# A Retention, MoE and feed-forward kernel: ring depth, task distances and forced work changed

## The chip, the cores and the metric

The kernel runs on one core of one Trainium2 chip. The metric is the device time of one execution in microseconds (us). Its engines are TensorE (PE for matmuls, PEld for its weight loads), VectorE (DVE), ScalarE (ACT), GpSimd (POOL) and SyncE (SP), which issues all DMAs here.

## What is computed

Three layers follow each other: Retention over 4 batches, 8 heads, 576 positions and 64 dims; a soft mixture of 8 experts whose mixing matrix P is normalised eight times by rows and columns; and a feed-forward layer with a leaky rectifier.

```python
ret = (1 / sqrt(64)) * (q @ k.T) * Dmat        # Dmat[i, j] = gamma_h ** (i - j), 0 above the diagonal
x = (ret @ v)                                  # 2304 tokens x 512
P = exp(x @ w_gate - max)
for _ in range(8):
    P /= P.sum(1, keepdims=True) + 1e-09
    P /= P.sum(0, keepdims=True) + 1e-09
    P *= N / E
x = sum(P[:, e:e + 1] * (maximum(x @ w1[e], 0) @ w2[e]) for e in range(8))   # 512 -> 1024 -> 512
h = x @ w_in                                   # 512 -> 2048
out = maximum(0.01 * h, h) @ w_out             # 2048 -> 512
```

## The kernel before

**Retention.** 20 chunks (`N`, loop over `n`) of 128 or 64 positions for two heads' halves. Each iteration loads q, k, v three and two chunks ahead, makes the scores on TensorE, multiplies them with the decay table on DVE (L640), adds the state's part, takes absolute values on ACT (L668) and sums them over a ones matrix. From that sum DVE makes a scale row `s` (L708), a power of two, and scales the output (L710). `keep_row` (L715) stores the row to memory two iterations later; `s` is a tile of a ring, two deep by its pool. POOL makes sums and differences of the scaled output (`emit_operands`), ACT and DVE split each into two 16-bit parts.

**Units.** The hidden width is cut into 20 units of 512 columns: 16 for the experts, 4 for the last layer (`NU1`, `NU`). A unit `u` goes over three stages `s` of 384 row pairs; a stage has 14 first products (`product_h`, seven in each of two halves `g`) and 15 groups of second products (`group_s`), which run 20 products behind. Every product is Strassen-like: seven products of operand sums, each of three matmuls on 16-bit parts. Units 0 and 15 (`PLAIN`) make their second products without it.

**Weights.** `prep_steps(u)` makes the tasks for a unit's weights: magnitudes, a scale (`top`, `scale`), scaling by it, then four `split`s: key `("w1", 0)` and `("w1", 1)` for the two halves of the first weights, `("w2",)` for both of the second. A split is twelve tasks: two casts on ACT, two differences and four sums on POOL, two casts on ACT, two differences on POOL. Unit 0's first weights are made during Retention, one task at a time from `step()`, of which an iteration has four. Its magnitudes are maxima on DVE and its scale uses a ones matrix; the other units take sums of magnitudes on ACT, transpose the column total on TensorE, take the maximum and broadcast it.

**The order.** Nothing is scheduled on the chip: `Order` writes the order of instructions at build time with a model of time. A task takes a fixed part and a part per element there, by engine (`COST`, L43); a gate step, entered with 1500 elements on DVE, is 1.75 us. Tasks lie in six queues; `pump` runs after each product and looks at the first 12 tasks of each queue (48 of "turn"). It emits those that are `ready`: every task they need has a modelled end at least `lat` back, their condition holds, their engine is nearly free. `flush` forces tasks whose time has come; `need` does it for weights, `need_x` for operands of a stage, `need_hid` for hidden values.

```python
def flush(self, name, want):
    q = self.queues[name]
    while any(want(x.key) for x in q):
        self.emit(q.pop(0))
```

So a forced task takes all that stands ahead of it in its queue with it. A half of the first weights has the condition `w1_free(g)`: the tile that it writes must have been read for the last time, for `g == 1` by the first half of the last stage of the unit before.

**Gate and layer change.** After the logits of the last stage, 11 tasks (`gate_steps`) normalise P on DVE, each with a product on TensorE for column sums. They must be done before unit 2's second products begin. After unit 15, `turn_steps` scales each row block on POOL (L1261), transposes it on TensorE (`turned`, L1271) and makes the operands of the last layer from it. In the last layer the leaky rectifier of two of the hidden blocks is one ACT instruction (`bent`, called from `splits` at L1057).

Of the kernel before, what the change touches and what calls it, by code (L numbers as in the profile page):

```python
# [8 lines left out]
F32 = mybir.dt.float32  # L9
F16 = mybir.dt.float16  # L10
BF16 = mybir.dt.bfloat16
# [19 lines left out]
ST = 384  # L31
# [4 lines left out]
WS = lambda u: 2.0 ** 13 if u else 2.0 ** 11  # L36
# [27 lines left out]
class Order:  # L64
# [43 lines left out]
    def flush(self, name, want):  # L108
        q = self.queues[name]
        while any(want(x.key) for x in q):  # L110
            self.emit(q.pop(0))
# [3 lines left out]
def retention_moe_ffn_kernel(ctx: ExitStack, tc: tile.TileContext, qk, vk, wg, wm, wf,  # L115
# [53 lines left out]
    def prep_steps(u, small_bank):  # L169
# [3 lines left out]
        def begin():  # L173
            st["iw"] = small.tile([P, 2], F32, tag="iw", name=f"iw{u}")
            st["m"] = small.tile([P, 2], F32, tag="m1f", name=f"m{u}") if u else \
                small.tile([P, 2], BF16, tag="m1b", name=f"m{u}", bufs=1)
# [3 lines left out]
        def amax(part, c):  # L180
            def f():
                nc.vector.tensor_reduce(st["mx"][:, part, c:c + 1], raws[u, part][:, 512 * c:512 * c + 512],
                                        axis=AX.X, op=ALU.max, apply_absolute_value=True)
            return f
# [6 lines left out]

        def top(p):
            def f():
                if u == 0:
                    nc.vector.reduce_max(st["m"][:, p], st["mx"][:, p], axis=AX.X)
                    return
                nc.vector.reduce_sum(st["m"], st["mx"], axis=AX.X)
                bk = small_bank(f"wt{u}")
                for part in range(2):
                    nc.tensor.matmul(bk[:1, P * part:P * part + P], st["m"][:, part:part + 1], ident,  # L200
                                     start=part == 0, stop=True, skip_group_check=True)
                st["r"] = small.tile([1, 2], F32, tag="mrw", name=f"mr{u}", bufs=1)
                nc.vector.reduce_max(st["r"], bk[:1, :2 * P].rearrange("p (a i) -> p a i", a=2), axis=AX.X)
            return f

        def scale(p):
            def f():
                bk = small_bank(f"ws{u}_{p.start}")[:, p]
                if u:
                    nc.tensor.matmul(bk, ones[:1, :], st["r"], start=True, stop=True)  # L210
                else:
                    nc.tensor.matmul(bk, ones_b, st["m"][:, p], start=True, stop=True)
                pow2(st["s"][:, p], bk, f"w{u}_{p.start}")
                recip2(st["iw"][:, p], st["s"][:, p])
                for part in range(p.start, p.stop):
                    s2 = st["s", part] = small.tile([P, 1], F32, tag=f"s2{part}", name=f"sw{u}_{part}", bufs=2)
                    nc.vector.tensor_scalar(s2, st["s"][:, part:part + 1], WS(u), None, op0=ALU.mult)
                if p.stop == 2:
                    fu = small.tile([P, 1], F32, tag="fu", name=f"fu{u}")
                    nc.vector.scalar_tensor_tensor(fu, st["iw"][:, 0:1], 1.0 / (XS * WS(u) ** 2 * HS), st["iw"][:, 1:2],  # L220
                                                   op0=ALU.mult, op1=ALU.mult)
                    wfac[u] = fu
            return f
# [69 lines left out]
        def maxes(part, key):  # L293
            there = None if u == 0 else lambda: (u, part) in raws and order.t >= raw_at[u, part] + 8
            return [add("A" if u else "D", 512, (mags if u else amax)(part, c), (first_,), key, there) for c in range(4)]

        def scaled(p, mx_, key):
            t_ = add("D", 40 if u == 0 else 400, top(p), mx_, key)
            return add("D", 500, scale(p), (t_,), key, lat=0.8)
# [46 lines left out]
        last0 = split(0, 0, pre0[0:2], ka, w1_free(0))  # L346
        pre1 = scales(1, sc, k2)
        last1 = split(1, 0, pre1[0:2], k2, w2_free) + split(1, 1, pre1[2:4], k2, w2_free)
        after(1, last1, k2)
        last0 += split(0, 1, pre0[2:4], kb, w1_free(1))  # L350
        after(0, last0, kb)
# [190 lines left out]
    with ExitStack() as actx:  # L542
# [146 lines left out]
        def emit_scale(n, bank=None):  # L689
# [9 lines left out]
            if c < 4:  # L699
# [3 lines left out]
                sv = s_t = awk.tile([P, P], F32, tag="s", name=f"s{n}")  # L703
# [71 lines left out]
        pre = prep_steps(0, lambda name: misc[0][:, 500:502] if misc[0] else idle_bank(name))  # L775
        wait, drain = [0], []
        emit_qk(0)
        for n in range(N):
# [19 lines left out]
            def step():  # L798
                wait[0] -= 2
                if n >= 4 and pre and pre[0].key == (0, "w1", 1) and wait[0] <= 0:  # L800
                    x = pre.pop(0)
                    wait[0] = {40: 8, 500: 4}.get(x.n, 2)
                    x.f()
                    x.done = 0.0
# [46 lines left out]
        misc[0] = None  # L851
# [89 lines left out]
    def bent(out_, in_, u, scale=1.0):  # L941
        if u < NU1:
            nc.scalar.activation(out_, in_, AF.Relu, scale=scale)
        else:
            nc.scalar.activation(out_, in_, AF.Prelu, scale=scale, alpha=SLOPE)

# [61 lines left out]
    def splits(u, s, g, what):  # L1008
# [45 lines left out]
        elif what == 1:  # L1054
            d = (evac[7], evac[3])
            if not moe:
                d = (add("A", 2 * ST, lambda: bent(fp[:, 1:3], fp[:, 1:3], u), d),)  # L1057
# [176 lines left out]
    def turn_steps(s, j0):  # L1234
# [52 lines left out]
        t = [add("AD", 512, turned(j, h), (b[h],) + p.get(f"x{h}", ()), 0.5) for h in range(2)]  # L1287
# [62 lines left out]
    for n, (u, s) in enumerate(stages):  # L1350
# [95 lines left out]
```

## Time and profile before

| | us |
|---|---|
| median of 3 runs | 1872.95 (1871.28 to 1875.13) |
| profiled execution | 1871.14 |
| its span, first to last instruction | 1869.4 |
| PE busy | 1798.8 (96%) |
| DVE busy | 1486.7 (80%) |
| ACT busy | 1262.1 (68%) |
| POOL busy | 814.7 (44%) |
| mean granted TensorE clock | 0.985 |

The share of busy time is a mean over stages. TensorE's own waits, its granted clock and what released each wait are read stretch by stretch. A granted clock of 1.00 is 2.4 GHz; a stretch below it ran partly at 1.2 GHz.

### The profile page before, as it was taken

To read this page: it belongs to the slowest core of one execution; us is meant where nothing else is said; L and a number is where in the kernel's file an instruction comes from. 1 tells how busy PE (TensorE), PEld (TensorE's weight loads), DVE (VectorE), ACT (ScalarE), POOL (GpSimd) and SP (SyncE) were. 2 spreads that over 40 slices of the span, in tenths; PEclk is the share of its full clock that TensorE was granted. 3 is DMA by queue.
4 is the path that set the end of the run, shared out by engine and by line. 5 is a ranking of instruction groups with operands and counts; after the bars stand their busy time and mean duration, and the time that the engine had idled before them with its cause. 6 is when DMAs were issued, how large, how long until landed. Compare 5 with 4: busy or idle time off the path is not lost.

```text
span 1869.4 us, 35931 instructions
## 1 busy us (share of the span) xinstructions
PE 1798.8 (96%) x13794; PEld 1301.0 (70%) x13794; DVE 1486.7 (80%) x2578; ACT 1262.1 (68%) x2645; POOL 814.7 (44%) x786
## 2 busy tenths in 40 slices
PE   8889999999999999999999999999999988999997
PEld 7744477777777777777777777777765556677776
DVE  7845587988988897988889898988766886597875
ACT  5656677677776767777776767676665666777653
POOL 4734362543525362544535352543227853263500
PEclk9899999999999999999999999999999999999999
DMA  8873353534454553544454453544433534344242
GB/s 321 302 249 102 121 152 122 182 114 150 147 165 135 156 161 118 182 127 148 140 177 132 142 169 123 175 134 129 125 114 104 184 118 142 116 116 148 83 121 77
DMA packets 207857, 276.67 MB, mean 148 GB/s; under 512 B 13874, under 2 KB 177860, under 8 KB 202564
## 3 DMA queue, kind: packets, MB, share of 16 engines
q1 hardware_dynamic: 207684, 274.37, 46.9%
q8 instruction: 108, 1.77, 0.4%
q14 instruction: 65, 0.53, 0.1%
HBM read 244.69 MB, written 29.63 MB: 147 GB/s over the span
## 4 chain that ended last, share of the span: by engine, by line
PE 81%; DVE 9%; POOL 4%; ACT 3%; DMA 2%; issue 2%; SPq 0%; DVEq 0%; ACTq 0%; POOLq 0%
PE s L1125 15%; PE hB L955 11%; PE hA L955 11%; PE s1a L1125 11%; PE hE L955 11%; PE s1b L1125 10%; PE hD L955 5%; DVE y L1138 2%; PE s L1167 2%; POOL raw L260 1%; DVE hs L1046 1%; PE s1b L1167 1%; PE s1a L1167 1%; DMA s_dram<-s 1%; POOL y L1261 1%
## 5 line engine op out<-in xcount | busy, mean ns | idle before, releaser
L955 PEld LDWEIGHTS <-w 128*128 128x128 f16 x5040 | 492.1, 98 | 269.5 <-issue 14.1
L1125 PEld LDWEIGHTS <-hs 128*128 128x128 f16 x3888 | 380.6, 98 | 92.9 <-DVE hs L1046 7.9
L1125 PEld LDWEIGHTS <-hp 128*128 128x128 f16 x2916 | 285.9, 98 | 90.6 <-issue 13.9
L253 POOL TENSOR_TENSOR w<-raw,w 128x384 f16<-128x384 f32 x152 | 164.5, 1096 | 331.2 <-ACT w L243 306.2
L260 POOL TENSOR_TENSOR raw<-raw 128x256 f32<-128x256 f32 x304 | 285.1, 938 | 20.2
L955 PE MATMUL hE<-x,w 128*128 128x384 f16 x1440 | 276.1, 328 | 5.2 <-DMA x<-x 2.8
L1138 DVE SCALAR_TENSOR_TENSOR y<-s,fac,y 128x256 f32<-128x256 f32 (+1 forms) x324 | 197.6, 612 | 102.4 <-PE s L1125 87.1
L955 PE MATMUL hB<-x,w 128*128 128x384 f16 x1440 | 275.1, 327 | 3.2 <-ACT hB L965 3.1
L955 PE MATMUL hA<-x,w 128*128 128x384 f16 x1440 | 276.8, 327 | 0.7 <-DMA x<-x 0.7
L1125 PE MATMUL s<-w,hs 128*128 128x256 f16 x1944 | 265.8, 273 | 1.0 <-ACT s L1143 1.0
L1046 DVE TENSOR_TENSOR hs<-fs,hs 128x768 f16<-128x768 f32 (+1 forms) x228 | 244.1, 1086 | 11.8 <-ACT hs L1036 11.6
L278 POOL TENSOR_TENSOR w<-raw,w 128x512 f16<-128x512 f32 x148 | 191.3, 1308 | 92.7 <-ACT w L272 92.4
L406 POOL TENSOR_TENSOR f<-f,e 128x256 f32<-128x256 f32 x64 | 53.4, 834 | 401.8 <-DVE e L398 393.3
L1036 ACT ACTIVATE hs<-fs 128x768 f16<-128x768 f32 (+1 forms) x228 | 187.6, 823 | 43.9 <-DVE fs L1071 24.6
L1036 ACT ACTIVATE hp<-fp 128x384 f16<-128x384 f32 x240 | 159.3, 678 | 27.6 <-DVE fp L994 20.4
L1138 DVE SCALAR_TENSOR_TENSOR y<-s1b,fac,y 128x512 f32<-128x512 f32 (+1 forms) x163 | 99.7, 612 | 51.1 <-ACT s L1143 22.3
L1125 PE MATMUL s1a<-w,hp 128*128 128x256 f16 x972 | 133.9, 274 | 6.5 <-DVE y L1138 3.5
L955 PE MATMUL hD<-x,w 128*128 128x384 f16 x720 | 139.7, 329 | 0.1
L1125 PE MATMUL s1a<-w,hs 128*128 128x256 f16 x972 | 134.8, 274 | 4.9 <-DVE hs L1046 3.7
L1125 PE MATMUL s1b<-w,hs 128*128 128x256 f16 x972 | 134.0, 273 | 5.1 <-ACT hs L1036 3.2
L1138 DVE SCALAR_TENSOR_TENSOR y<-s1a,fac,y 128x256 f32<-128x256 f32 (+1 forms) x161 | 98.3, 611 | 47.0 <-ACT s L1143 28.9
L1125 PE MATMUL s1b<-w,hp 128*128 128x256 f16 x972 | 132.7, 273 | 2.6 <-DVE y L1138 2.6
(198 smaller groups left out, 2689.9 us busy)
## 6 DMA issues: line engine op xcount, KB each, us to landing
x<-x SPq DMA_DIRECT2D x420, 384.0 KB, 4.1
raw<-in_wm SPq DMA_DIRECT2D x32, 1024.0 KB, 5.1
r<-in_wf SPq DMA_DIRECT2D x64, 256.0 KB, 2.8
qk<-in_qk SPq DMA_DIRECT2D x16, 512.0 KB, 5.9
vk<-in_vk SPq DMA_DIRECT2D x16, 512.0 KB, 5.2
wf_s<-f SPq DMA_DIRECT2D x32, 256.0 KB, 2.7
raw<-wf_s SPq DMA_DIRECT2D x8, 1024.0 KB
x<-xst SPq DMA_DIRECT2D x30, 256.0 KB, 2.0
```

Of the source, the lines that this page charges most:

```text
L253: nc.gpsimd.tensor_tensor(v[0], v[1], v[2], op=ALU.subtract)
L260: nc.gpsimd.tensor_tensor(o, x, y_, op=ALU.subtract)
L278: (nc.gpsimd if u or part else nc.vector).tensor_tensor(lo, r, hi, op=ALU.subtract)
L406: nc.gpsimd.tensor_tensor(dst, dst, cur["tx"].bitcast(F32), op=ALU.mult)
L955: nc.tensor.matmul(bank, w[:, a, wi, k, :], x[:, :, b, k, :], start=r in (1, 5) and k == q == 0, stop=k == 1 and q == 2, skip_group_check= ...
L1036: nc.scalar.activation(hid[k][:, 0, a:b], src[:, a:b], AF.Relu if moe and relu else AF.Copy)
L1046: nc.vector.tensor_tensor(t[:, 1, a:b], src[:, a:b], t[:, 0, a:b], op=ALU.subtract)
L1125: nc.tensor.matmul(out_, t[:, a, i, ts], w[:, b, wi, 0, :], start=start and k == 0, stop=k == 5, skip_group_check=True)
L1138: nc.vector.scalar_tensor_tensor(out_, bank, f, out_, op0=ALU.mult, op1=ALU.add)
L1167: nc.tensor.matmul(bank, t[:, a, i, ts], w[:, b], start=l == g == q == 0, stop=l == g == 1 and q == 2, skip_group_check=True)
L1261: nc.gpsimd.tensor_scalar(y[i], y[i], st["s", j][:, h:h + 1], None, op0=ALU.mult)
```

## The change

Seven edits. (1) The ring of Retention's scale rows is four deep. (2) Unit 0's weights are made as the other units' are, with magnitudes on ACT, and a task of them leaves `step()` once what it needs is two steps back (three for the maximum and the broadcast), chosen among the first six. (3) `top` is cut in two: the total on DVE (`total`), then transpose and maximum 0.6 us later in the model; the broadcast waits 1.2 instead of 0.8 us. (4) Gate steps wait 4.0 us of modelled time instead of 1.0. (5) The transposes at the layer change wait 1.5 instead of 0.5. (6) `flush` forces only the wanted tasks and what they depend on, and the second half of the first weights is queued ahead of the second weights. (7) The leaky rectifier of two blocks goes to ACT or DVE, whichever the model has free.

```diff
-WS = lambda u: 2.0 ** 13 if u else 2.0 ** 11
+WS = 2.0 ** 13
     def flush(self, name, want):
-        q = self.queues[name]
-        while any(want(x.key) for x in q):
-            self.emit(q.pop(0))
+        for x in list(self.queues[name]):
+            if want(x.key):
+                self.force(x)
+
+    def force(self, x):
+        for q in self.queues.values():
+            if x in q:
+                for d in x.deps:
+                    self.force(d)
+                q.remove(x)
+                self.emit(x)
+                return
...
+        def total(p):
+            def f():
+                nc.vector.reduce_sum(st["m"][:, p], st["mx"][:, p], axis=AX.X)
+            return f
         def top(p):
             def f():
-                if u == 0:
-                    nc.vector.reduce_max(st["m"][:, p], st["mx"][:, p], axis=AX.X)
-                    return
-                nc.vector.reduce_sum(st["m"], st["mx"], axis=AX.X)
-                bk = small_bank(f"wt{u}")
-                for part in range(2):
-                    nc.tensor.matmul(bk[:1, P * part:P * part + P], st["m"][:, part:part + 1], ident,
-                                     start=part == 0, stop=True, skip_group_check=True)
+                bk = small_bank(f"wt{u}_{p.start}")
+                n = p.stop - p.start
+                for i in range(n):
+                    nc.tensor.matmul(bk[:1, P * i:P * i + P], st["m"][:, p.start + i:p.start + i + 1], ident,
+                                     start=i == 0, stop=True, skip_group_check=True)
...
-            return [add("A" if u else "D", 512, (mags if u else amax)(part, c), (first_,), key, there) for c in range(4)]
+            return [add("A", 512, mags(part, c), (first_,), key, there) for c in range(4)]
         def scaled(p, mx_, key):
-            t_ = add("D", 40 if u == 0 else 400, top(p), mx_, key)
-            return add("D", 500, scale(p), (t_,), key, lat=0.8)
+            t_ = add("D", 10, total(p), mx_, key)
+            t_ = add("D", 300, top(p), (t_,), key, lat=0.6)
+            return add("D", 500, scale(p), (t_,), key, lat=1.2)
...
         last0 = split(0, 0, pre0[0:2], ka, w1_free(0))
+        last0 += split(0, 1, pre0[2:4], kb, w1_free(1))
+        after(0, last0, kb)
         pre1 = scales(1, sc, k2)
         last1 = split(1, 0, pre1[0:2], k2, w2_free) + split(1, 1, pre1[2:4], k2, w2_free)
         after(1, last1, k2)
-        last0 += split(0, 1, pre0[2:4], kb, w1_free(1))
-        after(0, last0, kb)
...
-                sv = s_t = awk.tile([P, P], F32, tag="s", name=f"s{n}")
+                sv = s_t = awk.tile([P, P], F32, tag="s", name=f"s{n}", bufs=4)
...
             def step():
-                wait[0] -= 2
-                if n >= 4 and pre and pre[0].key == (0, "w1", 1) and wait[0] <= 0:
-                    x = pre.pop(0)
-                    wait[0] = {40: 8, 500: 4}.get(x.n, 2)
-                    x.f()
-                    x.done = 0.0
+                wait[0] += 1
+                if n < 4:
+                    return
+                for x in pre[:6]:
+                    if x.key == (0, "w1", 1) and all(d in popped and wait[0] - popped[d] >= 2 + (x.n in (300, 500))
+                                                     for d in x.deps):
+                        pre.remove(x)
+                        popped[x] = wait[0]
+                        x.f()
+                        x.done = 0.0
+                        break
...
+    def bend(e, t, u):
+        if e is nc.scalar:
+            bent(t, t, u)
+        else:
+            nc.vector.scalar_tensor_tensor(t, t, SLOPE, t, op0=ALU.mult, op1=ALU.max)
...
-                d = (add("A", 2 * ST, lambda: bent(fp[:, 1:3], fp[:, 1:3], u), d),)
+                d = (add("AD", 2 * ST, lambda e: bend(e, fp[:, 1:3], u), d),)
...
-        t = [add("AD", 512, turned(j, h), (b[h],) + p.get(f"x{h}", ()), 0.5) for h in range(2)]
+        t = [add("AD", 512, turned(j, h), (b[h],) + p.get(f"x{h}", ()), 1.5) for h in range(2)]
...
-                        last = (Task("D", 1500, f, last, "gate", None, 1.0),)
+                        last = (Task("D", 1500, f, last, "gate", None, 4.0),)
```

## Rows read from the trace of the kernel before

**Rows 1.** Stretches: length, busy PE, PEld, DVE, ACT, POOL, then PEclk, DMA share, GB/s.
```profile
0.00:104.00 104.00, 86.15 (x1162) 75.92 (x1163) 74.83 (x135) 58.58 (x144) 57.33 (x62) 0.89 0.86 302
...
158.00:204.00 46.00, 39.92 (x214) 20.02 (x211) 35.41 (x92) 21.76 (x41) 27.20 (x30) 0.93 0.29 90
204.00:1340.00 1136.00, 1128.41 (x8538) 832.67 (x8536) 972.45 (x1677) 814.82 (x1706) 508.32 (x491) 1.00 0.48 146
...
1430.00:1615.00 185.00, 165.21 (x1006) 101.27 (x1004) 138.91 (x224) 118.70 (x251) 110.41 (x100) 0.94 0.46 147
1615.00:1840.00 225.00, 223.91 (x1714) 166.94 (x1712) 172.95 (x277) 152.76 (x302) 72.08 (x64) 1.00 0.36 107
```

**Rows 2.** DVE in order of time, Retention: start, us, what [idle before <-releaser].
```profile
24.36 0.29 DVE L708 TENSOR_SCALAR s<-l 128x128 int32<-128x128 int32 x1 [2.16 <-DMA s_dram<-s]
...
48.52 0.29 DVE L708 TENSOR_SCALAR s<-l 128x128 int32<-128x128 int32 x1 [1.85 <-DMA s_dram<-s]
...
100.62 0.29 DVE L708 TENSOR_SCALAR s<-l 128x128 int32<-128x128 int32 x1 [7.64 <-DMA s_dram<-s]
```

**Rows 3.** DMAs of the tile s_dram, the scale rows.
```profile
DMA to landing us min/median/max: 3.9/5.9/7.9
```

**Rows 4.** PE in order of time, Retention.
```profile
24.70 0.38 PE L736 MATMUL l<-gm,ones 128*128 128x1 f32 x2 [0.87 <-DVE s L708]
...
35.84 1.29 PE L637 MATMUL sc<-qk 64*128 64x128 f32 x14 [2.24 <-DVE w L640]
...
62.69 0.58 PE L697 MATMUL l<-ab,ones_b 128*128 128x128 bf16 x4 [4.13 <-ACT ab L668]
...
100.97 0.40 PE L697 MATMUL l<-ab,ones_b 128*128 128x64 bf16 x4 [4.70 <-DVE s L708]
```

**Rows 5.** ACT: a cast in order of time; then line 188's durations, all units.
```profile
60.06 1.14 ACT L272 CAST w<-raw 128x512 f16<-128x512 f32 x2 [2.71 <-POOL raw L260]
...
L188 ACT ACTIVATE junk<-raw x152: 608/629/635, 130.7 to 1699.6; 128x512 bf16<-128x512 f32 x152
```

**Rows 6.** PE at the gate, in order of time; then line 1157, the gate's first reader.
```profile
178.60 0.39 PE L902 MATMUL s1a<-cs,ones 128*128 128x8 f32 x2 [2.32 <-DVE cs L897]
...
193.19 0.39 PE L902 MATMUL s1b<-cs,ones 128*128 128x8 f32 x2 [3.01 <-DVE cs L897]
...
L1157 DVE TENSOR_SCALAR y<-y,prob x18: 465/478/1376, 320.9 to 398.9; 128x512 f32<-128x512 f32 x18
```

**Rows 7.** PE's waits, whole span: us in total, times, longest; the scales' lines.
```profile
PE s1a L1125 <- DVE mr L203: 3.0, 6, 0.5
...
PE s1a L200 <- DVE m L197: 2.6, 9, 0.7
...
PE s1b L200 <- DVE m L197: 1.9, 4, 0.7
```

**Rows 8.** PE's waits, whole span; the transposes' lines.
```profile
PE s1a L1271 <- POOL y L1261: 3.5, 4, 1.5
...
PE s1b L1271 <- POOL y L1261: 1.5, 2, 1.1
```

**Rows 9.** PE's waits, whole span; those for weights.
```profile
PE hE L955 <- POOL w L278: 1.6, 2, 0.9
...
PE hE L955 <- ACT w L272: 0.7, 1, 0.7
```

**Rows 10.** POOL in order of time: first and last differences of the same split.
```profile
855.52 1.83 POOL L253 TENSOR_TENSOR w<-raw,w 128x384 f16<-128x384 f32 x2 [1.14 <-ACT w L243]
...
939.62 0.92 POOL L253 TENSOR_TENSOR w<-raw,w 128x384 f16<-128x384 f32 x1 [0.96 <-ACT w L243]
...
949.13 2.28 POOL L278 TENSOR_TENSOR w<-raw,w 128x512 f16<-128x512 f32 x2 [1.91 <-ACT w L272]
```

**Rows 11.** A stretch of the layer change, columns as in rows 1.
```profile
1451.00:1523.00 72.00, 66.79 (x368) 35.91 (x367) 59.12 (x110) 44.27 (x98) 49.07 (x44) 1.00 0.53 174
```

**Rows 12.** Line 945 on ACT: durations, all units.
```profile
L945 ACT ACTIVATE fp<-fp x24: 827/842/847, 1491.6 to 1836.4; 128x768 f32<-128x768 f32 x24
```

More of the change, by code (lines that the diff above doesn't have):

```diff
@@ L174, in begin @@
             st["iw"] = small.tile([P, 2], F32, tag="iw", name=f"iw{u}")
-            st["m"] = small.tile([P, 2], F32, tag="m1f", name=f"m{u}") if u else \
-                small.tile([P, 2], BF16, tag="m1b", name=f"m{u}", bufs=1)
+            st["m"] = small.tile([P, 2], F32, tag="m1f", name=f"m{u}")
+            st["r"] = small.tile([1, 2], F32, tag="mrw", name=f"mr{u}", bufs=2)
             st["s"] = small.tile([P, 2], F32, tag="s12", name=f"s{u}")
             st["mx"] = small.tile([P, 2, 4], F32, tag="mx", name=f"mx{u}")
[L180 to L184, printed above, removed]
         def mags(part, c):
@@ L190, in mags @@
             return f
+        def total(p):
+            def f():
+                nc.vector.reduce_sum(st["m"][:, p], st["mx"][:, p], axis=AX.X)
+            return f
         def top(p):
             def f():
-                if u == 0:
-                    nc.vector.reduce_max(st["m"][:, p], st["mx"][:, p], axis=AX.X)
-                    return
-                nc.vector.reduce_sum(st["m"], st["mx"], axis=AX.X)
-                bk = small_bank(f"wt{u}")
-                for part in range(2):
-                    nc.tensor.matmul(bk[:1, P * part:P * part + P], st["m"][:, part:part + 1], ident,
-                                     start=part == 0, stop=True, skip_group_check=True)
-                st["r"] = small.tile([1, 2], F32, tag="mrw", name=f"mr{u}", bufs=1)
-                nc.vector.reduce_max(st["r"], bk[:1, :2 * P].rearrange("p (a i) -> p a i", a=2), axis=AX.X)
+                bk = small_bank(f"wt{u}_{p.start}")
[3 more added lines that the diff above has]
+                                     start=i == 0, stop=True, skip_group_check=True)
+                nc.vector.reduce_max(st["r"][:, p], bk[:1, :n * P].rearrange("p (a i) -> p a i", a=n), axis=AX.X)
             return f
@@ L208, in f @@
                 bk = small_bank(f"ws{u}_{p.start}")[:, p]
[L209 to L212, printed above, removed]
+                nc.tensor.matmul(bk, ones[:1, :], st["r"][:, p], start=True, stop=True)
                 pow2(st["s"][:, p], bk, f"w{u}_{p.start}")
@@ L216, in f @@
                     s2 = st["s", part] = small.tile([P, 1], F32, tag=f"s2{part}", name=f"sw{u}_{part}", bufs=2)
-                    nc.vector.tensor_scalar(s2, st["s"][:, part:part + 1], WS(u), None, op0=ALU.mult)
+                    nc.vector.tensor_scalar(s2, st["s"][:, part:part + 1], WS, None, op0=ALU.mult)
                 if p.stop == 2:
                     fu = small.tile([P, 1], F32, tag="fu", name=f"fu{u}")
-                    nc.vector.scalar_tensor_tensor(fu, st["iw"][:, 0:1], 1.0 / (XS * WS(u) ** 2 * HS), st["iw"][:, 1:2],
+                    nc.vector.scalar_tensor_tensor(fu, st["iw"][:, 0:1], 1.0 / (XS * WS ** 2 * HS), st["iw"][:, 1:2],
                                                    op0=ALU.mult, op1=ALU.mult)
@@ L773, in keeps @@
                 keep_x(0, *kept.pop(0))
-        pre = prep_steps(0, lambda name: misc[0][:, 500:502] if misc[0] else idle_bank(name))
-        wait, drain = [0], []
+        pre = prep_steps(0, lambda name: misc[0] if misc[0] else idle_bank(name))
+        wait, drain, popped = [0], [], {}
         emit_qk(0)
@@ L850, in retention_moe_ffn_kernel @@
         recip2(inv_of(1), inv_of(1))
-        misc[0] = None
+        misc[0], wait[0] = None, 0
         drain = [(1, rest(emit_scale, N - 1)), (1, last_rows),
```

## Prediction

> **What bounds the kernel now.** I read the table of stretches first [rows 1]. Its columns are length, then busy time of each engine, then TensorE's granted clock. TensorE is busy 1798.8 of 1869.4 us, so 70.6 us are idle, and what matters is where they lie. From 204 to 1340 us TensorE lacks 7.6 us in 1136, and from 1615 to 1840 us 1.1 in 225: there it is the bound and nothing can be had but those few us. Retention (0 to 104) lacks 17.9 us, the stretch of the gate (158 to 204) 6.1, the change of layers (1430 to 1615) 19.8. In these three the granted clock also has a mean of 0.89, 0.93 and 0.94, that is, parts of them ran at 1.2 instead of 2.4 GHz; each time that follows idle TensorE. The rest of the idle time (start of unit 0, unit 15, the tail) is 18 us. So the change can win in Retention, at the gate, at the change of layers and at the few us of the weights' scales, and can lose anywhere if it opens a new wait in the 1361 us that are now full.
>
> **Scale rows four deep.** DVE stood three times before the instruction that writes a scale row, for the DMA of the row two tiles earlier: 2.16, 1.85 and 7.64 us [rows 2]. The row's DMA takes 3.9 to 7.9 us to land, median 5.9 [rows 3], and an iteration of Retention is 86.15 / 20 = 4.3 us of TensorE work [rows 1]. With two tiles a row must be back about one iteration after it is issued, with four about three iterations after, 13 us against at most 7.9. All three waits go. TensorE lost 0.87 and 4.70 us behind the first and the third [rows 4]; the second costs it about one more, which I leave out. Gain 5.6 us gross. After the third, POOL's operand sums and ACT's copy come earlier too, so the first products of unit 0 follow and don't take the time back.
>
> The Trainium skill ("DMA: Bandwidth & Descriptors", Anatomy of one DMA) puts a small DMA's fixed cost at about 2.0 us, nearly all of it completion. By that figure a row would be back before an iteration is over, two tiles would do, and this edit would bring nothing: the sum below would end some 4 us higher. The rows decide: 3.9 at the least, because these rows share the DMA engines with the loads.
>
> **The first unit's weights by distance.** Four maxima leave DVE for ACT in Retention. They stood in front of the product with the decay table, and TensorE waited 2.24 us for that [rows 4]. ACT takes 4 x (0.63 us and a read of its accumulator) instead [rows 5]; it is busy 58.6 of 104 us, at most two of them in one iteration, so I cost them at nothing; without that cover up to 3 us. Each later step is now issued at least two steps behind what it needs. Before, ACT stood 2.71 us for POOL's sums [rows 5], and TensorE 4.13 us behind ACT [rows 4]; two steps are half an iteration, 2.1 us, at each of the four hand-overs of a split, so most of this should go. The chain total, transpose, maximum, broadcast adds under 1 us of TensorE per part; the three steps between keep it from waiting. Gain 6.4 us gross. Together 12.0 gross. What is late next are the loads: the DMA engines are 0.86 busy over these 104 us [rows 1], so only 14.6 us of them are free, and prefetch is two or three chunks deep. I take two thirds, **8 us**; bounds 0 (every us turns into a wait for loads) and 14.
>
> **Gate, latency 1.0 to 4.0.** Eleven steps are queued on DVE, each with a product on TensorE for the next. The planner books 1.75 us for one (`COST`), but the eleven fill this stretch, 46 / 11 = 4.2 us each, so TensorE reached a product too early and stood 2.32 and 3.01 us [rows 6], with the clock at 0.93 over the stretch. Idle 6.1 and clock loss 0.07 x 46 = 3.2: 9.3 us are to be had. Three us more per step put 5.6 to 6 us between steps, above every step's own time. The chain of ten gaps gets 30 us longer and ends near 234 us at the latest; its first reader starts at 320.9 us [rows 6], so the cover is 87 us. On DVE the gate lies beside other work: 35 us busy in 46 becomes less dense. I take **7.5**; bounds 2 and 9.3.
>
> **Weight scales further from TensorE.** In 19 units TensorE takes the column total from DVE right after DVE was given it. It stood 2.6 and 1.9 us before that product and 3.0 us before the next use of the bank [rows 7]. Now the total is its own step 0.6 us earlier, and the broadcast waits 1.2 instead of 0.8. The 4.5 should mostly go; the 3.0 stay, since the maximum still reads the bank. **3 us**; bounds 0 and 7.5.
>
> **Layer change: transposes at 1.5 instead of 0.5.** TensorE's transposes stood 3.5 and 1.5 us for POOL's scaling [rows 8], the longest 1.5. One us more covers all but the longest. Idle of this kind brings low clock with it; I count 5.0 idle minus 1 left plus 1 of clock, **5 us**. Against it: each of the three tiles of a stage reaches its store up to 1 us later, which is in the crowding term below. Bounds 0 and 7.
>
> **Forced work and the order of the halves.** Unit 17's second product with the second half of the first weights stood 1.6 and 0.7 us for that half's splits [rows 9]: `need` had to emit everything ahead in the queue, the second weights too, before it. With forcing by dependence and that half queued ahead, it is done before. With the clock behind it, **4 us**; bounds 0 and 5. Elsewhere forced lists held only what was wanted, so nothing.
>
> **What the new order costs.** This half may not start until the unit before has finished its last first-layer use, and it is exactly twelve tasks, the whole window that `pump` looks at. While it is shut, the second weights behind it are shut too. In the middle units they start later than now: the half's split runs from 939.62 to 951.41, 11.8 us, one unit after the same split at 855.52 [rows 10], so a unit is 84.1 us. From the opening to the first use of the second weights are 7 + 14 + 6 = 27 of a unit's 42 products, 54 us; three splits one behind the other are 35.4. It fits with 19 us over, TensorE stays fed, cost 0. At the change of layers the two splits of unit 16 used to lie ahead of 1451 and now fall between 1451 and 1523, where POOL is already busy 49.1 of 72 us [rows 11] with the scaling and the operand sums. Two splits are at most 23.6: 72.7 of 72. They can be late by a few us, or the operands of the next stage can. I take **5 us** lost; bounds 3 gained (POOL is freer before 1451) and 25 lost.
>
> **Leaky rectifier on ACT or DVE.** 24 pieces, 0.84 us each on ACT [rows 12]; whichever is free takes it. TensorE lacks 1.1 us in the stretch where most lie, so 0; bounds 1 gained, 3 lost where DVE, the busier one, takes it.
>
> **Sum.** 8 + 7.5 + 3 + 5 + 4 - 5 = 22.5. The profiled execution took 1871.14 us around a span of 1869.4; 1848.6 remains. The median of the runs shown is 1.8 us above that execution, so **1850 us**.
>
> **Rivals.** A: Retention is carried by its loads. For it: the share of 0.86; against it: TensorE's long waits were for DVE and ACT, not for loads. It gives back 6 of the 8 us: 1856. B: the spacing does nothing, because DVE and POOL lag the planner by more than the new distances; for it, a gate step of 4.2 us booked at 1.75. Gate, scales and transposes (15.5 us) are not won, and with the crowding at 8: 1869, no change to within what can be told. C, the other side: the second weights come late in every unit. For it: they stand behind a shut window, and then have to be made in one go beside a full DVE. Against it: 19 us of margin. It decides once the three splits need over 54 us, half again as long as now. Then each further us is paid in some 14 units, and 2 us late is 28 lost: 1878. The Trainium skill ("SBUF — State Buffer", SBUF: two separate sides) says that POOL and a DVE instruction with two SBUF inputs shut each other out for a whole instruction, which would speak for C. The trace agrees only in part: between 1451 and 1523 DVE's 59.1 and POOL's 49.1 busy us lie in 72, so at least 36 were side by side.
>
> **How the numbers follow.** Forecast 0.60 (its own range 1838 to 1861), A 0.12, B 0.16, C 0.12. The range to hold it 8 times in 10 reaches four fifths of the way to all better bounds (23.3 us better together, 1831) and up past B without C: 1831 to 1872. A measurement can tell about 0.2%, 3.7 us. Faster than 1869.2: forecast, A and half of B, 0.80; same 0.08; slower 0.12.
>
> **What would show it.** Right: no DVE wait for a scale row; a Retention that ends some 8 us before 104; a gate that ends near 220 to 234 with no wait over 1 us; no 0.7-us wait at the column totals; no wait for weights at unit 17. Wrong: ACT or TensorE waiting for qk and vk loads in Retention (A); gate waits of 2 us as before (B); waits for second weights at the start of a unit's second stage, or for operands at the last layer's stages (C and the crowding term).

## The result, and the profile after

| | before | after |
|---|---|---|
| median of 4 runs each, us | 1874.04 (1871.28 to 1875.57) | 1852.01 (1849.31 to 1855.54) |
| ratio | | 0.9885, 95% interval 0.9864 to 0.9907 |
| span of the profiled execution | 1869.4 | 1853.8 |
| mean granted TensorE clock | 0.985 | 0.988 |

The change is worth 22 us, 1.15%; 1850 was forecast. The profiled execution of after took 1855.54 us, the longest of its four, that of before 1871.14, less than any of the four. So the two traces differ by 15.6 us only.

First the stretches of after, which answer [rows 1]. Columns as there: length, busy PE, PEld, DVE, ACT, POOL, granted clock, DMA share, GB/s.

```profile
0.00:94.00 94.00, 80.61 (x1048) 71.88 (x1049) 65.97 (x121) 56.47 (x144) 49.98 (x56) 0.88 0.90 317
...
148.00:204.00 56.00, 56.00 (x344) 29.71 (x342) 38.05 (x92) 40.91 (x83) 32.21 (x35) 1.00 0.36 109
204.00:1340.00 1136.00, 1129.09 (x8572) 836.51 (x8570) 977.67 (x1703) 804.52 (x1686) 509.59 (x486) 1.00 0.47 145
...
1430.00:1600.00 170.00, 148.28 (x928) 92.53 (x926) 121.57 (x200) 113.23 (x234) 97.25 (x91) 0.96 0.45 142
1600.00:1825.00 225.00, 224.60 (x1723) 167.82 (x1721) 186.59 (x285) 151.24 (x309) 83.58 (x75) 1.00 0.38 112
```

The gate's stretch is full now: 56.00 busy of 56 us at full clock, where 39.92 of 46 stood at 0.93. Retention is not better: 13.4 us idle in 94, clock 0.88. The layer change still lacks 21.7 us.

To see where the 15.6 us come from, I take the end of each unit's last first products (`hD`) in TensorE's order of time in both traces, and subtract.

| stretch | before, us | after, us | difference |
|---|---|---|---|
| start to the second stage of unit 0 | 139.61 | 139.64 | 0.0 |
| to the end of unit 1 (the gate lies here) | 138.53 | 127.31 | -11.2 |
| units 2 to 13 | 1007.94 | 1003.28 | -4.7 |
| unit 14 | 91.28 | 94.23 | +3.0 |
| units 15 and 16 | 204.77 | 196.93 | -7.8 |
| unit 17 | 88.65 | 94.80 | +6.2 |
| unit 18 to TensorE's last product | 193.74 | 192.70 | -1.0 |

Then TensorE's waits over the whole span of after: what waited for what, us in total, times, longest.

```profile
PE sc L639 <- DVE w L642: 5.8, 2, 5.2
...
PE s1b L1284 <- POOL y L1274: 4.0, 2, 2.2
PE s1a L1138 <- DVE mr L207: 3.5, 7, 0.5
...
PE hA L968 <- ACT w L244: 2.3, 1, 2.3
PE l L699 <- DVE mr L207: 2.2, 1, 2.2
...
PE hE L968 <- ACT w L273: 2.0, 1, 2.0
...
PE s1a L205 <- DVE m L197: 0.8, 1, 0.8
```

Against [rows 7], the waits for the column total fell from 4.5 to 0.8 us, those for the maximum (`mr`) stayed. Against [rows 8], the waits for POOL's scaling went from 5.0 to 4.3. Against [rows 9], the waits for first weights did not go: 1.6 and 0.7 became 2.3 and 2.0 from ACT (and 1.7 from POOL). No second weights of a middle unit are waited for.

**Retention.** DVE no longer stands for a DMA before a scale row ([rows 2]: 2.16, 1.85 and 7.64 us). The landings in [rows 3] are not those of the rows: the view on `s_dram` has them from the loads that read the rows back (`inv<-s_dram`, L725). What the rows took is seen from the three waits of before. The stores that DVE stood for were issued (SP, start, us) at

```profile
17.66 0.31 SPq L717 DMA_DIRECT2D s_dram<-s  x1
...
44.76 0.28 SPq L717 DMA_DIRECT2D s_dram<-s  x1
...
93.44 0.28 SPq L717 DMA_DIRECT2D s_dram<-s  x1
```

and DVE went on at 24.36, 48.52 and 100.62: 6.7, 3.8 and 7.2 us later. But new waits came. Below, what answers [rows 4, 5], from ACT, DVE and TensorE in order of time (start, us, what, idle before).

```profile
37.37 0.38 PE L205 MATMUL l<-ident,m 128*1 128x128 f32 x2 [0.88 <-DVE s L710]
41.69 0.40 PE L699 MATMUL l<-ab,ones_b 128*128 128x128 bf16 x4 [2.24 <-DVE mr L207]
...
89.20 0.62 ACT L273 CAST w<-raw 128x512 f16<-128x512 f32 x1 [6.43 <-POOL raw L261]
89.86 1.09 DVE L279 TENSOR_TENSOR w<-raw,w 128x512 f16<-128x512 f32 x1 [5.84 <-ACT w L273]
...
91.60 1.11 PE L639 MATMUL sc<-qk 64*64 64x64 f32 x14 [5.21 <-DVE w L642]
```

The last three are one chain. A cast of the first unit's weights stands on ACT for POOL's sums (6.43). The difference that DVE makes from that cast was issued two steps later and stands on DVE for it (5.84). Behind it in DVE's queue is the product with the decay table, for which TensorE stands 5.21 us. The distance of two steps is too short for POOL, and an engine that the steps were to free is now blocked by one.

**Unit 17.** The scaling of unit 17's first weights (line 229 on ACT) was done last at 1563.80, while TensorE stood from 1562.70 on for their first half. The later of its two loads, issued by SP, the last magnitude and the last scaling of its first weights on ACT and the first difference on POOL, in order of time:

```profile
1500.89 0.32 SPq L176 DMA_DIRECT2D raw<-wf_s  x1
...
1545.35 0.61 ACT L191 ACTIVATE junk<-raw 128x512 bf16<-128x512 f32 x1
...
1563.80 0.72 ACT L229 ACTIVATE raw<-raw,sw 128x512 f32<-128x512 f32 x1
1565.00 1.78 POOL L254 TENSOR_TENSOR w<-raw,w 128x384 f16<-128x384 f32 x2 [42.92 <-ACT w L244]
```

This load, of the second weights' raw tile, left when POOL's last difference of unit 16's second weights was done (1499.70 and 1.16 us long); these weights now come behind the second half of the first ones. In the trace of before the later load, there of the other tile, left at 1481.63. The load is not all of it: the magnitude ahead of the last starts at 1523.36, so 22 us of the delay lie between two tasks whose data was there. From 1522 on POOL had nothing to do for 42.92 us.

### The profile page after: what moved, and what is told of

Read it like the earlier page. It is cut to its first block, busy times and chain, and to the rows that moved or that the text cites. A ratio compares the mean times of both kernels' runs of the same rounds, so it can differ in the third digit from the quotient of the medians.

```text
span 1853.8 us, 35942 instructions
## 1 busy us (share of the span) xinstructions
PE 1795.8 (97%) x13800; PEld 1303.5 (70%) x13800; DVE 1487.6 (80%) x2576; ACT 1261.7 (68%) x2659; POOL 823.9 (44%) x786
## 4 chain that ended last, share of the span: by engine, by line
PE 87%; DVE 6%; POOL 3%; ACT 1%; issue 1%; DMA 1%; SPq 0%; DVEq 0%; ACTq 0%; POOLq 0%
PE s L1138 16%; PE hB L968 12%; PE hA L968 12%; PE hE L968 12%; PE s1a L1138 11%; PE s1b L1138 11%; PE hD L968 6%; PE s L1180 2%; DVE y L1151 1%; PE s1a L1180 1%; PE sc L639 1%; PE s1b L1180 1%; PE xo L666 1%; DMA x<-x 1%; DVE xst L513 1%
## 5 line engine op out<-in xcount | busy, mean ns | idle before, releaser
L261 POOL TENSOR_TENSOR raw<-raw 128x256 f32<-128x256 f32 x304 | 281.3, 925 | 20.0
L279 POOL TENSOR_TENSOR w<-raw,w 128x512 f16<-128x512 f32 x148 | 200.4, 1369 | 72.3 <-ACT w L273 71.8
L1151 DVE SCALAR_TENSOR_TENSOR y<-s1a,fac,y 128x256 f32<-128x256 f32 (+1 forms) x161 | 98.6, 613 | 54.8 <-ACT s L1156 26.5
```

What stands on the lines that cost most here:

```text
L261: nc.gpsimd.tensor_tensor(o, x, y_, op=ALU.subtract)
L279: (nc.gpsimd if u or part else nc.vector).tensor_tensor(lo, r, hi, op=ALU.subtract)
L1151: nc.vector.scalar_tensor_tensor(out_, bank, f, out_, op0=ALU.mult, op1=ALU.add)
```

## The experiments

A kernel's median stands with its range; after is 1852.0 and before 1873.5 to 1874.1 in the four sets of runs. Stretches of unit ends are measured as in the table above.

**The ring alone,** on the kernel before.

```diff
-                sv = s_t = awk.tile([P, P], F32, tag="s", name=f"s{n}")
+                sv = s_t = awk.tile([P, P], F32, tag="s", name=f"s{n}", bufs=4)
```

> The kernel before with the ring of scale rows four deep and nothing else. Theory S (the ring does what was predicted, and the first unit's new way took it back): DVE's three waits for scale rows are gone, Retention ends about 5 us sooner than in the kernel before, 1868 us. Rival L (Retention is carried by its loads): the waits are gone, but waits for qk and vk loads take their place, and the time stays within 2 us of the kernel before, 1873 us.

Measured: 1866.41 (1863.03 to 1868.66), ratio 0.9964 [0.9952, 0.9976], 7.2 us by the medians; in the profile 6.0 at the second stage of unit 0, 6.4 through all middle units, 5.6 at the end. DVE doesn't stand for a row's DMA any more. Theory S holds; of rival L there is one wait of 1.9 us for `vk` at 97.19. What remains in Retention is what [rows 4, 5] had shown:

```profile
PE l L697 <- ACT ab L668: 7.9, 4, 5.7
```

This is the longest group of TensorE's waits up to 112 us in this kernel.

**The first unit as before,** on the changed kernel: maxima on DVE, the scale from a ones matrix, one task at a time in the old rhythm.

```diff
-WS = 2.0 ** 13
+WS = lambda u: 2.0 ** 13 if u else 2.0 ** 11
...
-            return [add("A", 512, mags(part, c), (first_,), key, there) for c in range(4)]
+            return [add("A" if u else "D", 512, (mags if u else amax)(part, c), (first_,), key, there) for c in range(4)]
...
-                for x in pre[:6]:
...
+                if n >= 4 and pre and pre[0].key == (0, "w1", 1) and wait[0] <= 0:
+                    x = pre.pop(0)
+                    wait[0] = {40: 8, 500: 4}.get(x.n, 2)
```

> The changed kernel with unit 0's weights made as before (maxima on DVE, the old spacing), all else changed. Theory S: the new way costs Retention about what the ring gains, so this ends some 4 us below the changed kernel, 1848 us, and the half clock from 40 to 60 us is gone. Rival L: Retention ends where it ended in both kernels, 1852 us. Prediction's own term (the new way gains 4 us): 1856 us.

Measured: 1851.08 (1850.12 to 1854.43), ratio 0.9887 [0.9872, 0.9901]: no difference from after that can be told. The wait for ACT is back, 8.5 us, and the one behind DVE's product with the decay table falls from 5.8 to 1.9. Its profile is 5.1 us ahead of before at the second stage of unit 0.

**The gate near,** on the changed kernel.

```diff
-                        last = (Task("D", 1500, f, last, "gate", None, 4.0),)
+                        last = (Task("D", 1500, f, last, "gate", None, 1.0),)
```

> The changed kernel with the gate's latency back at 1.0. Theory G (the gate's distance made the 12 us that the trace shows gained between 140 and 205 us): 1862 to 1864 us, with two or three waits of 2 to 3 us at the column sums and low clock behind them. Rival O (the gain there came from the second weights of unit 1, which the new order moved out of this stretch): 1852 to 1856 us, since POOL no longer slows the gate's DVE steps.

Measured: 1862.45 (1859.11 to 1864.56), ratio 0.9943 [0.9925, 0.996]: 10.4 us slower than after. The waits of [rows 6] are back. TensorE's waits from 140 to 235 us:

```profile
PE s1b L909 <- DVE cs L904: 3.5, 1, 3.5
PE s1a L909 <- DVE cs L904: 2.1, 1, 2.1
```

And the stretch of the gate, full in after, has 6.2 us idle:

```profile
148.00:204.00 56.00, 49.79 (x299) 25.38 (x297) 41.62 (x114) 32.05 (x64) 28.77 (x32) 0.97 0.29 88
```

In the traces after wins 9.0 us over this kernel between the second stage of unit 0 and the end of unit 1.

**The second weights queued ahead again,** on the changed kernel, forcing by dependences kept.

```diff
-        last0 += split(0, 1, pre0[2:4], kb, w1_free(1))
-        after(0, last0, kb)
         pre1 = scales(1, sc, k2)
         last1 = split(1, 0, pre1[0:2], k2, w2_free) + split(1, 1, pre1[2:4], k2, w2_free)
         after(1, last1, k2)
+        last0 += split(0, 1, pre0[2:4], kb, w1_free(1))
+        after(0, last0, kb)
```

> The changed kernel with the second weights queued ahead of the second half of the first weights again; forcing by dependence stays. Theory W (the new order alone makes the waits for weights at the start of unit 17): the 10 us lost between the ends of units 16 and 17's first half are not lost, units 0 to 16 lose 0 to 3 us, 1844 to 1847 us. Rival N (the waits at unit 17 come from the layer change itself, not from the order): within 2 us of the changed kernel, 1852 us. If the order made the gain at the gate (rival O of the run without the gate's distance), this is slower: 1858 us or more.

Measured: 1845.80 (1844.51 to 1849.15), ratio 0.9858 [0.984, 0.9876]: 6.2 us faster than after. Unit 14 and unit 17 don't lose any more (91.16 and 89.34 us instead of 94.23 and 94.80). The later of unit 17's two loads leaves at 1458.35 instead of 1500.89, and the scaling of its first weights is done 44 us earlier (1520.19 against 1563.80). Its last row on ACT, and the first cast of the split behind it:

```profile
1520.19 0.72 ACT L229 ACTIVATE raw<-raw,sw 128x512 f32<-128x512 f32 x1
1521.28 0.50 ACT L244 CAST w<-raw 128x384 f16<-128x384 f32 x1
```

Of TensorE's waits from 1535 to 1610 us only one is for weights (after: 6.0 us in four groups):

```profile
PE hE L968 <- POOL w L279: 1.9, 2, 1.1
```

The old order has a price of its own. From the second stage of unit 0 to the end of unit 1 this run takes 131.80 us, after 127.31: with the gate's distance unchanged TensorE stands there again. Its waits from 134 to 275 us:

```profile
PE s1b L909 <- DVE cs L904: 1.7, 1, 1.7
...
PE s1b L1180 <- DVE cs L910: 0.9, 1, 0.9
PE s1a L1180 <- DVE cs L910: 0.8, 1, 0.8
```

Unit 16 on its own gains 5.0 us, units 15 and 18 lose 2.2 and 2.0.

**Total and maximum in one task,** in all units but the first, on the changed kernel.

```diff
+            if u:
+                t_ = add("D", 400, lambda: (total(p)(), top(p)()), mx_, key)
+                return add("D", 500, scale(p), (t_,), key, lat=0.8)
```

> The changed kernel with the column total and the maximum of a weight scale in one task again, and the broadcast 0.8 instead of 1.2 us behind it, for all units but the first. Theory T: the split task wins about 5 us, most of it in the middle units, where the changed kernel gained 4.7 to 5.8 us on the kernel before from unit 2 to unit 13; without it the median is 1856 to 1858 and TensorE stands again about 0.5 to 0.7 us behind the column total, 4 us in all. Rival: the middle units gained by another edit, the order of the halves or the leaky rectifier; then 1852 and the gain over units 2 to 13 stays.

Measured: 1863.02 (1862.6 to 1868.47), ratio 0.9951 [0.9936, 0.9966]: 11 us slower than after, more than either theory said. But units 2 to 13 gain 4.1 us on before, nearly after's 4.7. TensorE's waits there are 2.4 us for the total and 1.5 for the broadcast instead of after's 3.0 for the maximum. The loss is one piece of 8.5 us in the first half of unit 15. From the chain of what ended last there (start, us, what):

```profile
1367.73 0.52 ACT e L396
1368.27 0.44 DVE e L403
1368.73 2.97 DMA r<-in_wf
1372.05 0.42 ACT f L391
1372.47 0.40 ACT e L396
1372.87 0.39 ACT hB L981
```

ACT copies an accumulator (`hB`) only after the conversion of the last layer's weights from 64 to 32 bits, pieces that hand on between DMA, DVE, ACT and POOL. In after ACT's last piece starts at 1307.8 us; here it starts at 1372.0, and three lie in the last 5.3 us. The edit itself touches none of it: the planner placed it elsewhere.

**The transposes near,** on the changed kernel.

```diff
-(b[h],) + p.get(f"x{h}", ()), 1.5)
+(b[h],) + p.get(f"x{h}", ()), 0.5)
```

> The changed kernel with the transposes at the layer change 0.5 us behind POOL's scaling, as before. Theory of the prediction: the distance of 1.5 us wins 5 us, so 1857 here, with POOL's scaling ending 5 us of TensorE's waits. Rival: POOL lags the planner by more than 1.5 us there, so the distance hides little; TensorE still stood 4 us behind POOL's scaling in the changed kernel; then 1852, within 1.5 us.

Measured: 1848.87 (1847.54 to 1852.62), ratio 0.9872 [0.9858, 0.9887]: not slower, if anything 3 us faster. In the profile units 15 and 16 gain 3.5 us on before, after 7.8: where it acts the distance is worth 4.4. Unit 17 then takes 88.66 us instead of 94.80. The new order stands in this kernel, and the later load of unit 17 leaves at 1496.16, only 4.7 us sooner than in after. But the last magnitude starts at 1522.75 instead of 1545.35, and the first weights are scaled by 1546.9 instead of 1564.5. So the late load alone does not make unit 17 late.

**Old order and old forcing together:** as the run with the second weights ahead, and:

```diff
-        for x in list(self.queues[name]):
-            if want(x.key):
-                self.force(x)
+        q = self.queues[name]
+        while any(want(x.key) for x in q):
+            self.emit(q.pop(0))
```

> The changed kernel with the second weights queued ahead of the second half of the first weights, and with the old way of forcing, all that stands ahead in the queue. The run with the old order alone took 1845.8. Theory of the prediction: forcing by dependences alone is worth up to 4 us at unit 17, so 1849 to 1850 here, with TensorE standing 2 us for weights there. Rival: with the old order little stands ahead of what is forced, so the way of forcing is worth under 1 us: 1846.

Measured: 1848.04 (1845.62 to 1848.97), ratio 0.9863 [0.9848, 0.9877], against 1845.80; the intervals overlap, and the traces differ by 0.7 us at the end, in favour of this one. The way of forcing is worth nothing that can be told once the old order stands.

**Old order, and four steps behind a task of POOL.**

```diff
-wait[0] - popped[d] >= 2 + (x.n in (300, 500))
+wait[0] - popped[d] >= 2 + (x.n in (300, 500)) + 2 * (d.eng == "G")
```

> The old order of the halves as in the run of 1845.8, and in Retention a task of the first unit's weights leaves four steps, not two, behind a task of POOL that it needs. Theory: two steps are too few for POOL's sums, which held ACT for 6.4 us, DVE for 5.8 and TensorE for 5.2 at the end of Retention in the changed kernel; with four, these waits go and Retention ends 3 to 5 us earlier: 1841 to 1843. Rival: the time of Retention is then set by something else, its loads or the longer chain of tasks that no longer fits before unit 0; then 1846 or up to 3 us more.

Measured: 1841.75 (1838.04 to 1845.38), ratio 0.983 [0.9811, 0.9849]. The wait behind DVE falls to 0.3 us, so the theory holds in what it said of the chain. A new wait, for POOL's `qd`, stands in its place, probably because POOL's weight tasks now lie between Retention's own.

```profile
PE xo L656 <- POOL qd L616: 9.1, 6, 2.2
```

This is TensorE's longest group of waits up to 110 us. The six are short, and the granted clock from 0 to 94 us is 0.98 (after: 0.88).

**Old order, and the first unit as before:** the edits of those two runs together.

> The old order of the halves (1845.8 alone), and the first unit's weights made as in the kernel before: maxima on DVE, one task at a time in a fixed rhythm. Theory of the prediction: the new way is worth two thirds of 6.4 us, so 1850 here, and TensorE stands again 4 to 8 us behind the absolute values on ACT. Rival: the new way only moves that wait to DVE's scale chain and the second split, and is worth nothing; then 1844 to 1847, with a shorter Retention in the profile, not a longer one.

Measured: 1840.77 (1838.97 to 1842.49), ratio 0.9829 [0.9812, 0.9845]: 5.0 us faster than the old order alone. At the second stage of unit 0 it is 4.5 us ahead of it, with TensorE's waits up to 112 us:

```profile
PE l L710 <- ACT ab L681: 5.9, 4, 3.3
PE xo L677 <- DMA vk<-in_vk: 3.6, 1, 3.6
```

So the first unit's new way loses, with the old order of the halves: it takes these 5.9 us behind ACT down to 1.4 and brings 5.4 behind DVE's product with the decay table and 2.2 behind the scale's chain. Another 4.4 us lie behind Retention: to the end of unit 1 this run takes 127.44 us against 131.80, and the gate's waits of the old order alone are gone. The wait for `vk` is the longest for a load in Retention, after 1.9 us with the ring alone and 0.7 with the first unit as before: rival A's kind.

**Four steps, and the transposes near:** the edits of those two runs together.

> The version of 1841.75 (old order, four steps behind POOL's tasks) with the transposes again 0.5 us behind POOL's scaling. The same edit on the changed kernel took nothing, 1848.9 against 1852, but its unit 17 moved by 8 us, so the stretch before it must be read alone: there 4.6 us were lost. Theory: the distance of 1.5 us is worth about 4 us, which shows where unit 17 isn't disturbed: 1845 to 1847, and the loss lies between 1330 and 1550 us. Rival: it is worth nothing; 1841 to 1843.

Measured: 1853.47 (1851.76 to 1856.38), ratio 0.9895 [0.988, 0.991]: 11.7 us slower than with 1.5 us. Units 15, 16 and 17 lose 4.0, 4.4 and 3.9 us. Waits from 1410 to 1660 us:

```profile
PE s1a L1284 <- POOL y L1274: 5.8, 6, 2.1
PE s1a L1138 <- ACT hs L1049: 4.3, 2, 4.1
PE hE L968 <- ACT w L273: 3.2, 1, 3.2
PE hE L968 <- DMA x<-x: 2.7, 1, 2.7
```

The first is the edit's own; with 1.5 us it is 1.8. The other three stand behind other tasks; that these moved with it is likely and was not followed up.

**Old order, and the scale's task joined:** the edits of those two runs together.

> The old order of the halves (1845.8 alone), with total and maximum of a weight scale in one task again and the broadcast 0.8 us behind it. With the new order the split task won only half a microsecond over units 2 to 13, since 3.0 us of waits for the maximum took the place of 2.4 for the total. Theory: with the old order it takes both away, 4.6 us of TensorE's waits between 285 and 1280 us, so 1850 to 1851 here and waits of 4 to 5 us there. Rival: the split task is worth under 1 us here too, and the old order alone took the waits away: 1845 to 1847.

Measured: 1850.54 (1848.17 to 1853.0), ratio 0.9878 [0.9863, 0.9893]: 4.7 us slower than the old order alone. From unit 2 to unit 13 it loses 6.9 us. TensorE's waits from 285 to 1280 us:

```profile
PE s1a L1141 <- DVE mr L207: 3.0, 6, 0.5
PE s1a L205 <- DVE m L197: 1.7, 6, 0.7
```

In the same stretch of the old order alone all that is left of them is:

```profile
PE s1b L205 <- DVE m L197: 0.6, 1, 0.6
```

The theory holds: with the old order the split task takes both waits away, with the new one it trades one for the other.

**Four steps, and the leaky rectifier on ACT alone,** as it was before.

```diff
-                d = (add("AD", 2 * ST, lambda e: bend(e, fp[:, 1:3], u), d),)
+                d = (add("A", 2 * ST, lambda: bent(fp[:, 1:3], fp[:, 1:3], u), d),)
```

> The version of 1841.75 with the leaky rectifier of two blocks on ACT alone, as before. Prediction: the free choice of the engine is worth 0, between 1 gained and 3 lost; 1841 to 1843 here. Rival: it matters in the last layer, where DVE is the busier engine; then 1839 without it, or 1845 and above if ACT is what TensorE waits for there.

Measured: 1868.28 (1866.48 to 1870.45), ratio 0.9974 [0.9964, 0.9984]: 26.5 us slower. Up to unit 15 the two traces are alike (0.5 us); units 16, 17 and 18 lose 6.7, 12.2 and 7.2. In the old order unit 17's second weights stand ahead of the second half of its first. The last scaling of the second weights on ACT, then a cast of that half's split and POOL's last differences:

```profile
1564.71 0.72 ACT L229 ACTIVATE raw<-raw,sw 128x512 f32<-128x512 f32 x1
...
1588.93 1.14 ACT L273 CAST w<-raw 128x512 f16<-128x512 f32 x2 [5.75 <-POOL raw L261]
1589.63 2.27 POOL L279 TENSOR_TENSOR w<-raw,w 128x512 f16<-128x512 f32 x2 [0.73 <-ACT w L273]
```

With the free choice 13 of the 24 pieces go to DVE, and that scaling starts at 1542.96, 22 us sooner; magnitudes end within a microsecond of 1478 in both. Of the 22 us, 13 are there before ACT comes in: TensorE makes the broadcast of the scale (L213) at 1510.51 instead of 1497.66. Nor is ACT fuller: from 1490 to 1566 us it is busy 46.9 us here and 54.3 with the free choice. So unit 17's weights are late because the tasks stand in another order; which entry of the planner's model moved them is not shown.

## Why the prediction was right, and where it was not

The total, its sign and its range held. The terms did not hold so well; their errors cancelled, so that the sum came out within 2 us is in good part luck. (The better bounds of the terms add up to 24.3 us and not 23.3; the leaky rectifier's 1 was left out. Four fifths still end at 1831.)

**Retention, 8 forecast; 0.0 in the profile of after, 1.7 to 4.7 in three others with the same Retention.** The ring is right as put: 5.6 gross, 7.2 measured alone, no wait of DVE for a row left. The step that sized it read the wrong DMAs: 3.9 to 7.9 us are landings of the loads of `inv`. The rows themselves took 3.8 to 7.2 us in the three waits of before, so the comparison with one and with three iterations comes out the same. By the fixed cost of about 2.0 us that the Trainium skill gives ("DMA: Bandwidth & Descriptors", Anatomy of one DMA), two tiles would have done. The figure is given there for DMAs that GpSimd issues; SyncE issues these, and the 3.8 to 7.2 us decide. The step that failed is "two steps are half an iteration ..., so most of this should go": a sum on POOL comes far later than that, and the step behind it blocks DVE, not only ACT. The first unit's term is -0.9 (within what can be told) on the changed kernel and -5.0 with the old order (by the traces 4.5 in Retention and 4.4 at the gate, some of it lost again later), not a part of 6.4 won. What four profiles with the same Retention (after, gate near, scale joined, transposes near) leave open is its size: they reach the second stage of unit 0 at 139.64, 136.05, 137.96 and 134.96, against before's 139.61. Units 2 to 13 repeat to 0.01 us in three of them (-4.66, -4.65, -4.65 against before). So the 6.4 us by which the traces of before and after differ less than the medians are likely to lie up to 4.7 in Retention and 1.7 in unit 14 (94.23 us in after, 92.55 to 92.64 in the other three); that is argued, not shown.

**Gate, 7.5 forecast; 9.0 in the traces, 10.4 by the medians.** The mechanism is right: the gate ends at 221 us as forecast (220 to 234), and the longest wait left is 0.5 us. The size was low because I took 1.8 off the 9.3 to be had for steps that would still be late; none is. The medians go beyond the bound of 9.3. But the distance does it together with the new order: with the old one, 1.7, 0.9 and 0.8 us of waits are left and the stretch is 4.5 us longer, a gain of the new order that I had not seen.

**Scales, 3 forecast.** "The 3.0 stay" is what after shows. But its value hangs on the order of the halves: half a microsecond in the middle units with the new order, 6.9 there (4.7 in all) with the old. The 11 us of the joined task on the changed kernel are mostly a displaced conversion.

**Transposes, 5 forecast; 4.4 in units 15 and 16 where the new order stands, 8.3 where the old does.** On the whole time it is nothing or -3 in the one and 11.7 in the other. The step is right for its own stretch; "covers all but the longest" wasn't, since 4.3 us of waits for POOL remain in after.

**Forced work, 4 forecast.** The step that failed is that the half, "queued ahead, ... is done before": it is unit 17's first weights as a whole that come late, and TensorE's waits for them grew. Forcing itself is worth nothing that could be told, with the old order; it was not undone with the new one.

**The new order, -5 forecast; -6.2 by the medians; by the traces 8.5 lost in units 14 and 17, 5.0 in unit 16 and 4.5 won at the gate.** Sign and size are right, the place is not. I looked for it in POOL's crowding between 1451 and 1523, late second weights and late operands. In fact a raw tile is held longer and the later load of unit 17 leaves late, at 1500.89 us. I costed that edit by POOL's busy time and not by who holds the tile that the next unit's load needs. The held tile is not the whole cause: with the transposes near it is held nearly as long (1496.16) and unit 17 loses nothing. The rest is 22 us between the last two magnitudes of after; what placed them so is open.

**Leaky rectifier, 0 forecast, bounds 1 gained and 3 lost; 26.5 gained** where it was undone, in the version with the old order and four steps. I argued from TensorE's 1.1 us of idle time in the stretch where most pieces lie, in a kernel in which ACT carried them all. The 13 pieces in question are 10.9 us of ACT at 0.84 each; the rest of the loss, like the late scaling of unit 17, comes with another order of tasks, in which ACT is not fuller. Whether it is as much on the changed kernel was not run.

**Rivals.** C didn't come: no middle unit waits for second weights. The 36 us of DVE and POOL side by side, its last argument, are spans, and these may hold waiting: POOL's difference L253, always the same shape, took 905 to 1892 ns in before. B didn't come either. A shows only in part, where the ring is four deep and the first unit made as before (1.9, 0.7 and 3.6 us for `vk`).

**No sum.** The single undoings on the changed kernel give 10.4, 11.0, -3.1, -0.9 and -6.2, which with the ring's 7.2 are 18.4 and not 22.0, and three of them (first unit, scales, transposes) have another value beside the other order. Both versions with the old order and a mended first unit, 1840.77 and 1841.75, beat before by 32 to 33 us and after by 10 to 11.

## What to carry to other kernels

Where a planner writes the order of instructions, a small edit has two prices: its own wait, which the trace of before shows, and a displacement of whatever the planner now places elsewhere, which here was as large (8.5 us behind a conversion, 6 us at unit 17, 26 us in units 16 to 18). Read the effect in the stretch where the edit acts, and try it beside at least two orders before it is judged. Before a task is queued ahead of another, ask who waits for the buffer that the other one holds.

## What the runs showed of the chip that was not expected

The clock of Retention differs from profile to profile, and not by the wait ahead of it alone. In after TensorE stands 2.24 us before 41.69; then come these stretches (columns as in [rows 1]):

```profile
40.00:50.00 10.00, 8.31 (x92) 7.29 (x94) 6.19 (x15) 4.97 (x9) 4.67 (x6) 0.68 0.91 330
50.00:60.00 10.00, 10.00 (x96) 9.01 (x96) 7.88 (x14) 6.47 (x17) 4.69 (x5) 0.50 0.83 271
```

With the second weights ahead it stands 2.2 us at the same place, and then:

```profile
40.00:50.00 10.00, 7.76 (x115) 6.72 (x114) 8.18 (x17) 6.21 (x13) 6.66 (x7) 1.00 0.90 295
50.00:60.00 10.00, 8.39 (x143) 7.35 (x144) 9.60 (x17) 6.48 (x17) 4.13 (x5) 1.00 0.98 358
```

In after TensorE was at 1.2 GHz for part of the first ten us and all of the second, though idle for only 1.7 us of the twenty; by an estimate from these shares the same work would take 0.32 x 8.31 + 0.50 x 10.00 = 7.7 us less at full clock. In the other kernel it was idle for 3.85 us and stayed at 2.4 GHz. The kernel with the scale joined went like after (0.65 and 0.50), those with the gate near and the transposes near kept 1.00 behind a wait of 1.7 us. What decides isn't shown by these traces.
